# Batch 0's Z: filled by SBUF to SBUF transfers instead of through a DRAM scratch

## The chip, the cores and the metric

The kernel runs on one core of a Trainium2 chip. The metric is the device time of one execution in microseconds, as the median of several runs. Times inside the kernel come from one profiled execution and count from its first instruction. PE is TensorE, DVE is VectorE, ACT is ScalarE, POOL is GpSimd, SP is the queue that issues most transfers.

## The reference

`x` has 8 batches of 3008 rows and 256 columns. A frequency mixing is followed by an expert layer with ELU:

```python
X = np.fft.rfft(x, axis=1)
Yr = Xr @ w_r - Xi @ w_i + b_r
Yi = Xr @ w_i + Xi @ w_r + b_i
Y  = soft_threshold(Yr, 0.01) + 1j * soft_threshold(Yi, 0.01)
y  = np.fft.irfft(Y, n=3008, axis=1)
h  = y.reshape(8 * 3008, 256) @ w_in          # 256 x 2048
g  = np.where(h > 0, h, np.exp(np.minimum(h, 0)) - 1)
out = g @ w_out                               # 2048 x 256
```

## The kernel before

The sequence length is 3008 = 47 x 64. The forward transform of a batch has two steps. In step A, 64 rows of `x` (n2) for each of 47 column indices n1 are multiplied by the matrix `M1`; n1 is taken in 24 pairs (j and j + 23), one on each half of the 128 partitions, so that one product with `M1` gives 128 rows: a pair, two parts (32 cosine-like and 32 sine-like slots each). Six units A of four pairs each load their pairs from one of three tiles `xts` (two units a tile), write a PSUM tile and are copied to an SBUF tile `A` in bf16. In step X, a slot k of `Z` has the rows of all n1 on the partitions: `Z[p, k, :]`, and its product with `M2[:, k]` gives the frequencies in `XT`. Between the two, the axis n1 has to move from the free dimension to the partitions. That is done through a scratch in DRAM: unit A stores its tile to `DA` (L184 for batch 0, one store for each unit; L186 for the others), and `load_Z` (L192) reads `DA` back with 32 partitions a transfer, `Z[a:P:4]` for a = 0 to 2 (partitions with a = 3 are cleared once, by ACT, in `clear_Z`). For batch 0 the reads are cut at slots 8 and 16, so that the first units X (unit g, dt: 8 slots, one half of D) can start on the first slots.

Then come the units M (L254: four matmuls of `XT` with `wcat_r` and `wcat_s`, 128 rows of `Y` each; the bias comes through `bias_bc` or through a matmul with `bias_p` that starts the sum), the soft threshold (ACT Relu and DVE, or POOL), the inverse transform (B: L446, `DB` in DRAM, `Bs`, Y: L531), and the expert layer in blocks of 512 rows: front (L1032, L1044), ELU (L1083, L1073) and back (L1104).

All instructions of an engine run in the order in which the program writes them (a manual schedule). Batch 0's transform stands alone at the start; the transforms of the later batches are spread between the steps of the expert layer by `plan(b)`. The lines of the start, in program order:

- `idle_pe(n)` (L573) issues n matmuls on a constant that keep PE busy and whose result is not used.
- POOL issues the six loads of `x` for batch 0 (L118), SP those of `w_r`, `w_i` and the biases. Constants follow from iotas: `M1` (L689, L690 on DVE, of the Sin at L684), then `M2` in two halves g = 0, 1: `points`, `wraps`, `sizes`, `signs` on DVE (L731 to L761) and `sines` on ACT (L764); `slot0` (L776) scales M2's slot 0. `M3` follows from `v3`, `w3` and `a3` (L841 to L849 on DVE) by Sin on ACT (L917); POOL makes M4's inputs, `idm` and two casts of `wcat` (L780 to L801).
- `fA(u)` for u = 0 to 5: unit A of batch 0, then three idle matmuls. The PSUM tile of unit 5 is two banks (`apart`), copied by ACT and DVE.
- the seven `load_Z`, with the bias (through `bpd` in DRAM) between them; `idle_pe(26)`; the product that gives `bias_bc` (L854, L855).
- `load_w_in(0)` on SP; on POOL a `gate` that waits for a slot of Z, then the three loads of batch 1's `x` and half of `w_out` (L879).
- eight units X, evacuated by ACT (even) and DVE (odd, the last by both).
- `begin_M`, `first_M` and `fB` in a written order; `load_w_in(1)` is issued by SP after the store of `fB(3)`, and the scalings of `w_in` (L884) stand between the other steps of DVE.

Of the kernel before, what the change touches and what calls it, by code (L numbers as in the profile page):

```python
# [19 lines left out]
N1 = 47  # L20
# [9 lines left out]
def kernel(  # L30
# [112 lines left out]
    def evac(dst, src, on_dve):  # L143
        if on_dve:
            nc.vector.tensor_copy(dst, src)
        else:
            nc.scalar.copy(dst, src)  # L147

    def unit_A(b, u, alone=False, on_dve=False, apart=False):
# [12 lines left out]
        xt, A = xts[ci], A_of[b, ci]  # L162
        dav = DA_of[b].rearrange("j p d -> p j d")
# [6 lines left out]
        for j in range(2):  # L170
            nc.tensor.matmul(  # L171
                banks[j], lhsT=M1[:],
                rhs=xt[:, 4 * uu + 2 * j : 4 * uu + 2 * j + 2, :], start=True, stop=True,
            )
        Af = A[:, 4 * uu : 4 * uu + 4, :].rearrange("p n d -> p (n d)")
        if apart:
            for j in range(2):
                evac(Af[:, 512 * j : 512 * j + 512], banks[j], on_dve and bool(j))
        else:
            evac(Af, ps[:].rearrange("p a b -> p (a b)"), on_dve)  # L180
        j0 = 8 * ci
        if alone:
            j0 += 4 * uu
            nc.sync.dma_start(dav[:, j0 : j0 + 4, :], A[:, 4 * uu : 4 * uu + 4, :])  # L184
        elif uu == 1:
            nc.sync.dma_start(dav[:, j0 : j0 + 8, :], A[:])  # L186
# [7 lines left out]
    def unit_X(b, u, alone=False, on_dve=False, apart=False):  # L194
# [10 lines left out]
        for kk in range(8):  # L205
            k = 8 * g + kk
            nc.tensor.matmul(  # L207
                psv[kk // nk][:, kk % nk, 0 : 4 * K1], lhsT=Z[:, k, dt * P : dt * P + P],
                rhs=M2[:, k].rearrange("p c m -> p (c m)"), start=True, stop=True,
            )  # L210
# [365 lines left out]
    nc.vector.memset(bias_p[:], 0.0)  # L576
    bpd = dram.tile([3, 2 * D], BF16, name="bpd", tag="bpd")
# [5 lines left out]
    with tc.tile_pool(name="stagep", bufs=1) as stagep:  # L583
        def first_x(u):
            load_x(0, u // 2, 4 * (u % 2), 4 * (u % 2) + 4)
# [17 lines left out]
        w_r_f, w_i_f = (wk3.tile([P, 2, D], F32, name="yb", tag="yb") for _ in range(2))  # L603
        nc.sync.dma_start(w_r_f[:], w_r.rearrange("(c p) e -> p c e", p=P))
        nc.sync.dma_start(w_i_f[:], w_i.rearrange("(c p) e -> p c e", p=P))
        bsm = stagep.tile([8, D // 4], F32, name="bsm")
# [16 lines left out]
        def row(name, shape):  # L623
            return stagep.tile(shape, F32, name=name)
# [62 lines left out]
        c0 = col(dve, c1, -1.0, ALU.mult, 1.0, ALU.add)  # L687
        M1v = M1[:].rearrange("p (h k) -> p h k", h=2)
        dve.tensor_scalar(M1v[:, 0], r1[:], c0[:], None, ALU.mult)  # L689
        dve.tensor_scalar(M1v[:, 1], r1[:], c1[:], None, ALU.mult)  # L690

# [35 lines left out]

        def points(g):

            for t in range(2):  # L730
                dve.tensor_tensor(  # L731
                    v2[g][:, :, :, t], band(uw, t, 16 * g, 16),
                    kt[:, :, t].unsqueeze(1).to_broadcast([P, 16, K1]), ALU.add,
                )
# [43 lines left out]

        for k in range(3):
            pool.tensor_copy(bps[:, k], bsm[:])  # L780
            if k < 2:
                pool.tensor_tensor(bsm[:], bsm[:], bps[:, k], ALU.subtract)
        k4h = col(pool, qcol, 0.5, ALU.mult, -0.25, ALU.add)
# [3 lines left out]
        pool.tensor_tensor(c4[:], qcol[:], k42[:], ALU.subtract)  # L787
        nc.gpsimd.memset(lam_n[:], -LAM)
        nc.gpsimd.memset(hpi[:], 0.25 * TURN)
        ph4 = col(pool, c4, 0.25, ALU.mult, 0.25, ALU.add)  # L790
# [10 lines left out]
        pool.tensor_copy(wcat_s[:, :, D : 2 * D], w_r_f[:])  # L801

        def fA(u):
            unit_A(0, u, alone=True, on_dve=u == 5, apart=u == 5)
            if u < 5:
                idle_pe(3)

        points(0)
        wraps(0)
        sizes(0)  # L810
        signs(0)
        points(1)
        dve.tensor_scalar(m3i[:], m3i[:], 63, None, ALU.bitwise_and)
        k3 = row("k3", [P, NV])
        dve.scalar_tensor_tensor(k3[:], m3i[:], float(N1), k1t[:], ALU.mult, ALU.add)
        dve.tensor_scalar(sg3[:], k3[:], S // 2 + 0.5, -0.5, ALU.is_gt, ALU.add)
        full = [P, NV, N2]
        k3b = k3[:].unsqueeze(2).to_broadcast(full)
        for u in range(4):
            fA(u)  # L820
        nc.sync.dma_start(bpd[:].rearrange("k (q e) -> q k e", q=8), bps[:])
        fA(4)
        fA(5)
        ips.append(pre1.tile([P, 512], F32, name="ips", tag="mps1"))
        load_Z(0, 0, 0, 16)
        for k in range(3):
            nc.sync.dma_start(bias_p[32 * k : 32 * k + 1, :], bpd[k : k + 1, :])
        load_Z(0, 1, 0, 16)
        load_Z(0, 2, 0, 8)
        load_Z(0, 2, 8, 16)  # L830
        for a in range(3):
            load_Z(0, a, 16, NS)
        sines(0, 0)
        sines(0, 1)
        wraps(1)
        slot0()
        sines(1, 0)
        nc.scalar.activation(a2[1][:], v2[1][:], AF.Abs)
        nc.scalar.copy(wcat_r[:, :, D : 2 * D], w_i_f[:])
        nc.scalar.activation(wcat_s[:, :, 0:D], w_i_f[:], AF.Copy, scale=-1.0)  # L840
        dve.scalar_tensor_tensor(  # L841
            v3[:], n2row.unsqueeze(1).to_broadcast(full), 1.0 / S, k3b, ALU.mult, ALU.mult
        )
        signs(1)
        sines(1, 1)
        nc.scalar.activation(r4[:], v4[:], AF.Sin, bias=0.0, scale=TURN)
        dve.tensor_scalar(w3[:], v3[:], CMAGIC, -CMAGIC, ALU.add, ALU.add)
        dve.tensor_tensor(w3[:], v3[:], w3[:], ALU.subtract)
        dve.tensor_scalar(  # L849
            a3[:].bitcast(I32), w3[:].bitcast(I32), 0x7FFFFFFF, None, ALU.bitwise_and  # L850
        )
        nb = pre1.tile([P, 512], F32, name="ips", tag="mps1")
        idle_pe(26)
        nc.tensor.matmul(nb[:], lhsT=busy[:, 0:P], rhs=bias_p[:], start=True, stop=True)  # L854
        nc.scalar.copy(bias_bc[:], nb[:])  # L855

# [57 lines left out]
    for q, i in ((3, 0), (3, 1), (4, 1), (5, 1)):  # L914
        begin_M(q, i, pre2, "pre2")
    for o, src, sc, bi in ((1, w3, TURN, 0.0), (0, a3, -TURN, hpi[:])):
# [395 lines left out]
```

## Time and profile before

| | us |
|---|---|
| median of 3 runs (lowest, highest) | 879.21 (878.71, 880.23) |
| the profiled execution | 879.04 |
| its span, first to last instruction | 877.2 |
| PE busy | 862.8 (98%) |
| ACT busy | 713.9 (81%) |
| DVE busy | 664.2 (76%) |
| POOL busy | 583.4 (67%) |

A row of the timeline has the start, the length, the engine, the line, the operation, the tiles out and in, the shape and the count; in brackets stands the idle time of the engine before it and what ended it. Rows of the chain that ended last have start, length, engine, tile and line. Rows of groups have busy time and mean nanoseconds of one, then idle time before. Rows of stretches have from and to, the length, then busy time (and instructions) of PE, weight loads, DVE, ACT and POOL, the granted clock, the DMA share and GB/s.

### The profile page before, as it was taken

How to read it: one execution, taken by the hardware profiler on the slowest of the kernel's cores; microseconds unless marked ns; L12 is line 12 of the kernel's file. 1: busy time of each engine (PE TensorE's matmuls, PEld its weight loads, DVE VectorE, ACT ScalarE, POOL GpSimd, SP SyncE). 2: the span in 40 equal slices, each digit the busy share in tenths (PEclk: the TensorE clock that was granted, in tenths of full speed). 3: DMA queues.
4: the chain of work that ended last, by engine and by line, in shares of the span. 5: the costliest groups of instructions: out<-in, count | busy, mean ns of one | idle time of the engine just before them, and what ended most of it. 6: DMA issues, size and time to landing. Idle time of an engine off the chain costs nothing.

```text
span 877.2 us, 18462 instructions
## 1 busy us (share of the span) xinstructions
PE 862.8 (98%) x6731; PEld 670.2 (76%) x6731; DVE 664.2 (76%) x1106; ACT 713.9 (81%) x1248; POOL 583.4 (67%) x856
## 2 busy tenths in 40 slices
PE   7899999999999999999999999999999999999997
PEld 3467767877778877887778877787877878787776
DVE  7698778787776877768867788677777677788775
ACT  6777888888978889798887988879888798876664
POOL 7462550798757887578756888469874697734664
PEclk9999999999999999999999999999999999999999
DMA  8998337643383324733365532653337313250111
GB/s 255 330 260 239 98 96 200 186 133 85 97 264 122 97 73 122 240 121 108 89 179 162 162 104 79 176 175 128 101 82 229 87 33 91 73 145 25 38 37 49
DMA packets 118098, 117.69 MB, mean 134 GB/s; under 512 B 11651, under 2 KB 108934, under 8 KB 114486
## 3 DMA queue, kind: packets, MB, share of 16 engines
q1 hardware_dynamic: 111750, 88.97, 35.6%
q0 software_dynamic: 5968, 27.26, 9.8%
q8 instruction: 53, 0.87, 0.4%
q14 instruction: 39, 0.32, 0.1%
q10 hardware_dynamic: 288, 0.26, 0.1%
HBM read 54.86 MB, written 49.81 MB: 119 GB/s over the span
## 4 chain that ended last, share of the span: by engine, by line
PE 93%; POOL 2%; DVE 2%; ACT 1%; DMA 1%; SPq 1%; issue 0%; DVEq 0%; POOLq 0%
PE ps_o L1104 39%; PE hps L1032 33%; PE mps L296 5%; PE aps L171 2%; PE xps L207 2%; PE mps L1032 2%; PE yps L558 2%; PE bps L397 2%; PE mps L254 2%; PE sps L1032 1%; POOL Y L312 1%; DMA Z<-DA 1%; POOL yb L308 0%; PE ips L573 0%; POOL clip L311 0%; PE pre L254 0%
## 5 line engine op out<-in xcount | busy, mean ns | idle before, releaser
L1073 DVE SCALAR_TENSOR_TENSOR gT<-Et,hps 128x512 fp32r<-128x512 f32 x610 | 390.2, 683 | 135.7 <-POOL Et L1083 125.8
L1104 PE MATMUL ps_o<-w_out_r,gT 128*128 128x256 f32 x3008 | 477.3, 301 | 0.0
L1104 PEld LDWEIGHTS ps_o<-w_out_r,gT 128*128 128x128 f32 x3008 | 404.4, 189 | 48.2 <-DVE osb L1116 0.2
L1083 POOL TENSOR_SCALAR Et<-Et 128x512 f32<-128x512 f32 x482 | 288.0, 617 | 208.0 <-ACT Et L1044 206.3
L1032 PE MATMUL hps<-yT,w_in_s 128*128 128x512 bf16 (+7 forms) x1580 | 355.8, 352 | 0.9 <-DVE gT L1073 0.8
L1044 ACT ACTIVATE Et<-hps 128x512 f32<-128x512 f32 x494 | 271.5, 609 | 38.6 <-PE hps L1032 35.5
L1032 PEld LDWEIGHTS <-w_in_s 128*128 128x128 bf16 x1728 | 144.1, 98 | 104.9 <-issue 13.1
L1042 ACT ACTIVATE Et<-hps 128x512 f32<-128x512 f32 x192 | 104.5, 597 | 42.0 <-PE hps L1032 41.5
L1047 ACT ACTIVATE Et<-Et 128x512 f32<-128x512 f32 x192 | 110.5, 632 | 0.0
L312 POOL TENSOR_TENSOR Y<-yb,clip 128x512 bf16<-128x512 f32 x72 | 92.8, 1288 | 6.0
L308 POOL TENSOR_TENSOR yb<-yb,bias_bc 128x256 f32<-128x256 f32 x72 | 53.3, 740 | 11.2 <-DVE yb L303 11.2
L147 ACT CAST XT<-xps 128x768 bf16<-128x768 f32 x58 | 46.6, 805 | 15.9 <-PE xps L207 15.8
L303 DVE TENSOR_TENSOR yb<-mps,yb 128x512 f32<-128x512 f32 x72 | 49.8, 692 | 7.2
L147 ACT CAST yT<-yps 128x752 bf16<-128x752 f32 x56 | 44.1, 788 | 13.7 <-PE yps L558 13.5
L1075 DVE SCALAR_TENSOR_TENSOR gT<-hps,Et 128x512 fp32r<-128x512 f32 x78 | 50.2, 686 | 3.3
L147 ACT CAST A<-aps 128x1024 bf16<-128x1024 f32 x41 | 41.8, 1020 | 12.9 <-PE aps L171 11.0
L311 POOL TENSOR_SCALAR clip<-yb 128x512 f32<-128x512 f32 x72 | 44.3, 615 | 6.3
L147 ACT CAST Bz<-bps 128x1024 bf16<-128x1024 f32 x41 | 41.5, 1013 | 5.4 <-PE bps L397 5.1
L302 DVE TENSOR_TENSOR yb<-mps,bias_bc 128x256 f32<-128x256 f32 x72 | 30.5, 424 | 17.5 <-PE mps L296 15.7
L296 PE MATMUL mps<-wcat_s,XT 128*128 128x256 bf16 x288 | 43.2, 273 | 0.0
L1116 DVE COPY osb<-ps_o 128x512 f32<-128x512 f32 x46 | 31.7, 690 | 5.3 <-PE ps_o L1104 3.4
L224 POOL TENSOR_TENSOR XS<-XT 128x512 bf16<-128x512 bf16 x30 | 34.1, 1162 | 2.4 <-ACT XT L147 1.4
(201 smaller groups left out, 691.6 us busy)
## 6 DMA issues: line engine op xcount, KB each, us to landing
xt<-in_x_dram POOLq DMA_DIRECT2D x21, 1024.0 KB, 5.4
out_dram<-osb SPq DMA_DIRECT2D x158, 128.0 KB
Bs<-DB SPq DMA_DIRECT2D x30, 384.0 KB
Yx<-Y SPq DMA_DIRECT2D x168, 64.0 KB
DA<-A SPq DMA_DIRECT2D x19, 512.0 KB
DB<-Bz SPq DMA_DIRECT2D x19, 512.0 KB
Z<-DA SPq DMA_DIRECT2D x21, 384.0 KB
xt<-in_x_dram POOLq DMA_DIRECT2D x6, 512.0 KB, 8.2
```

Of the source, the lines that this page charges most:

```text
L147: nc.scalar.copy(dst, src)
L296: nc.tensor.matmul(out_, lhsT=lhs[:, dt] if lhs is not None else sum_of(dt, ch)[:, oc : oc + P], rhs=w[:, dt, :], start=(dt == 0), stop=(d ...
L308: nc.gpsimd.tensor_tensor(yb[:, D : 2 * D], yb[:, D : 2 * D], bias_bc[:, D : 2 * D], ALU.add)
L312: nc.gpsimd.tensor_tensor(Y_of[b, q][:, i, :], yb[:], clip[:], ALU.subtract)
L1032: nc.tensor.matmul(hps[s][:, c0:c1], lhsT=w_in_s[:, dt, ft * P : ft * P + P], rhs=yT_of[b][:, dt, t0 : t0 + c1 - c0], start=(dt == 0), sto ...
L1042: nc.scalar.activation(Et[:, s], hps[s], AF.Relu, scale=-1.0)
L1044: nc.scalar.activation(Et[:, s], hps[s], AF.Exp)
L1047: nc.scalar.activation(Et[:, s], Et[:, s], AF.Exp, scale=-1.0)
L1073: nc.vector.scalar_tensor_tensor(o, e, -1.0, h, ALU.add, ALU.max)
L1075: nc.vector.scalar_tensor_tensor(o, h, 0.0, e, ALU.max, ALU.add)
L1083: nc.gpsimd.tensor_scalar(e, e, 1.0, 0.0, ALU.min, ALU.max)
L1104: nc.tensor.matmul(po[q][:, i_ % 2, :], lhsT=gT[:, s, i_ * P : i_ * P + P], rhs=w_out_r[:, ft, :], start=(ft == 0 and i_ % 2 == 0), stop=( ...
```

## The change

- For batch 0, each unit A now multiplies by `M1c` instead of `M1`: a column pair's product is made by two accumulating matmuls of 256 columns, each with weights that are zero except on 64 of the 128 rows of the result, so that the two n1 pairs of a "t" share a PSUM bank by slots. A unit is eight matmuls of 256 columns instead of two of 512.
- The result of each half unit (t = 0, 1) goes from `A` straight into Z: `place(t)` writes 8 partitions (r0, r0 + 4, ... r0 + 28), 32 slots of 256 each, from 128 partitions of 512 elements. SP issues one of the two, POOL the other. `DA`, its stores and the seven `load_Z` are gone for batch 0; the slots of Z are interleaved for it, which `unit_X` undoes by its index.
- Every slot of Z now needs all twelve transfers; the `gate` before batch 1's loads is gone. `M1`, for the later batches, is made by two ACT instructions.
- Around it the start is rewritten: idle matmuls 1 (3 after unit 1) between the units and 16 after them; `w_r` and `w_i` are loaded after the placements; the bias goes from SBUF to `bias_p` without `bpd`; `w3` moves from DVE to POOL, in front of batch 1's loads; `sines(1, 1)` moves behind the first unit X; the `w_i` parts of `wcat` and `bias_bc` move behind the units X; the Sin of `r4` moves behind the first units M; the last unit X uses one tile.

The diff, cut to what matters:

```diff
-            if ci == 0:
+            if ci == 0 and not alone:
                 DA_of[b] = dram.tile([NJ, P, D], BF16, name="DA", tag="DA")
...
+        if alone:
+            for t in range(2):
+                for q in range(2):
+                    for j in range(2):
+                        nc.tensor.matmul(
+                            banks[t][:, D * q : D * q + D],
+                            lhsT=M1c_of[0][:, q, N2 - N2 * j : N2 - N2 * j + P],
+                            rhs=xt[:, 4 * uu + 2 * t + j, :], start=(j == 0), stop=(j == 1),
+                        )
...
+        def place(t):
+            r0 = 16 * (4 * uu + 2 * t) + ci
+            eng = nc.gpsimd if t == by_pool else nc.sync
+            eng.dma_start(Z[r0 : r0 + 29 : 4], Af[:, 512 * t : 512 * t + 512])
+
+        by_pool = 0 if apart else 1
...
-        if alone:
-            j0 += 4 * uu
-            nc.sync.dma_start(dav[:, j0 : j0 + 4, :], A[:, 4 * uu : 4 * uu + 4, :])
...
-                lhsT=Z[:, k, dt * P : dt * P + P],
+                lhsT=Z[:, k if b else 2 * (k % 16) + k // 16, dt * P : dt * P + P],
...
-        if b == 0:
+        if b == 0 and (q, i) != (3, 0):
             todo.sort(key=lambda z: z[1])
...
+        M1c = stagep.tile([P, 2, 3 * N2], F32R, name="M1c")
+        nc.vector.memset(M1c[:].bitcast(F32), 0.0)
...
+        r1v = r1[:].rearrange("p (q a b) -> p q a b", q=2, a=2)
+        for h, c in enumerate((c0, c1)):
+            dve.tensor_scalar(
+                M1c[:, :, N2 + NS * h : N2 + NS * h + NS].rearrange("p a (q b) -> p a q b", q=2),
+                r1v, c[:], None, ALU.mult,
+            )
...
+        def fA(u):
+            unit_A(0, u, alone=True, on_dve=u == 5, apart=u == 5)
+            if u < 5:
+                idle_pe(3 if u == 1 else 1)
...
+        points(1, (0,))
+        for u in range(3):
+            fA(u)
+            split_bias(u)
+            if u == 1:
+                for h, c in enumerate((c0, c1)):
+                    nc.scalar.activation(M1[:, N2 * h : N2 * h + N2], r1[:], AF.Copy, scale=c[:])
+        fA(3)
         k4h = col(pool, qcol, 0.5, ALU.mult, -0.25, ALU.add)
         k4 = col(pool, k4h, CMAGIC, ALU.add, -CMAGIC, ALU.add)
         k42 = col(pool, k4, 2.0, ALU.mult)
+        fA(4)
+        fA(5)
         c4 = stagep.tile([P, 1], F32, name="c4z")
         pool.tensor_tensor(c4[:], qcol[:], k42[:], ALU.subtract)
...
         pool.tensor_scalar(idm[:], prow, pcol[:], None, ALU.is_equal)
+        ips.append(pre1.tile([P, 512], F32, name="ips", tag="mps1"))
+        nc.sync.dma_start(w_r_f[:], w_r.rearrange("(c p) e -> p c e", p=P))
+        nc.sync.dma_start(w_i_f[:], w_i.rearrange("(c p) e -> p c e", p=P))
         pool.tensor_copy(wcat_r[:, :, 0:D], w_r_f[:])
         pool.tensor_copy(wcat_s[:, :, D : 2 * D], w_r_f[:])
...
         for k in range(3):
-            nc.sync.dma_start(bias_p[32 * k : 32 * k + 1, :], bpd[k : k + 1, :])
...
+            nc.sync.dma_start(bias_p[32 * k : 32 * k + 1, :], bps[:, k])
+        points(1, (1,))
         sines(0, 0)
         sines(0, 1)
         wraps(1)
+        sizes(1)
         slot0()
         sines(1, 0)
...
         signs(1)
...
-        idle_pe(26)
...
+        idle_pe(16)
...
     load_w_in(0)
-    gate(Z[:, 8, 0:1])
+    nc.gpsimd.tensor_scalar(w3[:], v3[:], CMAGIC, -CMAGIC, ALU.add, ALU.add)
+    nc.gpsimd.tensor_tensor(w3[:], v3[:], w3[:], ALU.subtract)
     for ci in range(3):
         load_x(1, ci)
     load_w_out(0)
     for u in range(8):
-        unit_X(0, u, alone=True, on_dve=u % 2, apart=u == 7)
+        unit_X(0, u, alone=True, on_dve=u % 2)
         if u < 3:
             idle_pe(1)
+        if u == 0:
+            sines(1, 1)
+    nc.scalar.copy(wcat_r[:, :, D : 2 * D], w_i_f[:])
+    nc.vector.tensor_scalar(wcat_s[:, :, 0:D], w_i_f[:], -1.0, None, ALU.mult)
...
     for q, i in ((3, 0), (3, 1), (4, 1), (5, 1)):
         begin_M(q, i, pre2, "pre2")
+    nb = pre1.tile([P, 512], F32, name="mps1", tag="mps1")
+    nc.tensor.matmul(nb[:], lhsT=busy[:, 0:P], rhs=bias_p[:], start=True, stop=True)
+    nc.scalar.copy(bias_bc[:], nb[:])
+    nc.vector.tensor_scalar(
+        a3[:].bitcast(I32), w3[:].bitcast(I32), 0x7FFFFFFF, None, ALU.bitwise_and
+    )
...
     first_M(4, 0, False)
+    nc.scalar.activation(r4[:], v4[:], AF.Sin, bias=0.0, scale=TURN)
```

More of the change, by code (lines that the diff above doesn't have):

```diff
@@ L147, in evac @@
             nc.scalar.copy(dst, src)
+    M1c_of = []
     def unit_A(b, u, alone=False, on_dve=False, apart=False):
@@ L169, in unit_A @@
             banks = [ps[:, j, :] for j in range(2)]
[L170 to L175, printed above, removed]
+        if alone:
[7 more added lines that the diff above has]
+                        )
+        else:
+            for j in range(2):
+                nc.tensor.matmul(
+                    banks[j], lhsT=M1[:],
+                    rhs=xt[:, 4 * uu + 2 * j : 4 * uu + 2 * j + 2, :], start=True, stop=True,
+                )
[4 more added lines that the diff above has]
+        by_pool = 0 if apart else 1
         if apart:
@@ L726, in band, with points @@
             )
-        def points(g):
-            for t in range(2):
+        def points(g, ts=(0, 1)):
+            for t in ts:
                 dve.tensor_tensor(
@@ L776, in slot0, with split_bias @@
                     dve.tensor_scalar(w, w, cc[:], None, ALU.mult)
-        for k in range(3):
+        nc.gpsimd.memset(lam_n[:], -LAM)
+        nc.gpsimd.memset(hpi[:], 0.25 * TURN)
+        def split_bias(k):
             pool.tensor_copy(bps[:, k], bsm[:])
@@ L782 @@
                 pool.tensor_tensor(bsm[:], bsm[:], bps[:, k], ALU.subtract)
+        def fA(u):
+            unit_A(0, u, alone=True, on_dve=u == 5, apart=u == 5)
+            if u < 5:
+                idle_pe(3 if u == 1 else 1)
+        points(0)
+        wraps(0)
+        sizes(0)
+        signs(0)
+        dve.tensor_scalar(m3i[:], m3i[:], 63, None, ALU.bitwise_and)
+        k3 = row("k3", [P, NV])
+        dve.scalar_tensor_tensor(k3[:], m3i[:], float(N1), k1t[:], ALU.mult, ALU.add)
+        dve.tensor_scalar(sg3[:], k3[:], S // 2 + 0.5, -0.5, ALU.is_gt, ALU.add)
+        full = [P, NV, N2]
+        k3b = k3[:].unsqueeze(2).to_broadcast(full)
+        dve.scalar_tensor_tensor(
+            v3[:], n2row.unsqueeze(1).to_broadcast(full), 1.0 / S, k3b, ALU.mult, ALU.mult
+        )
+        points(1, (0,))
[6 more added lines that the diff above has]
+        fA(3)
         k4h = col(pool, qcol, 0.5, ALU.mult, -0.25, ALU.add)
```

68 lines of the change are left out of this document (14 added, 54 removed).

## The prediction

> **What bounds the kernel now.** I read the page first (the chain by engine), then the busy time by stretches, then the chain of the first 60 us, and last the timeline of the stages that the diff touches.
>
> ```profile
> span 877.2 us, 18462 instructions
> ...
> PE 93%; POOL 2%; DVE 2%; ACT 1%; DMA 1%; SPq 1%; issue 0%; DVEq 0%; POOLq 0%
> 24.00:31.00 7.00, 4.51 (x71) 3.30 (x69) 3.96 (x6) 4.20 (x7) 2.94 (x5) 1.00 0.83 265
> ...
> 31.00:44.00 13.00, 13.00 (x93) 5.84 (x91) 8.57 (x14) 10.36 (x18) 7.50 (x8) 1.00 1.19 380
> ...
> 100.00:800.00 700.00, 699.82 (x5558) 557.69 (x5556) 531.25 (x859) 594.00 (x1038) 485.62 (x675) 1.00 0.44 127
> ```
>
> The first numbers of each stretch are its length and the busy time of PE. From 100 to 800 us PE is full; the diff changes nothing there, so whatever the start wins or loses arrives at the end. The start has one hole: 2.5 us of PE between 24 and 31. From 31 to 44 PE is full and the DMA engines are too (share 1.19, 380 GB/s). The profiled execution took 879.04 us, of which 877.2 are the span; the median of the three runs is 879.21. I sum against 879.04. A measurement of this kernel can tell about 0.2% (1.76 us) from no change.
>
> ```profile
> 10.99 0.85 PE aps L171 x2
> ...
> 11.84 1.31 PE ips L573 x3
> ...
> 14.80 0.47 PE aps L171 x2
> ...
> 23.65 4.56 DMA Z<-DA
> ...
> 53.51 0.94 PE ps_o L1104 x8
> ```
>
> These are rows of the chain: start, length, what. Batch 0's Z is the hole: the last read back from DRAM ends at 28.2.
>
> **The A products.** A unit was two fp32 matmuls of 512 columns, 0.85 us at half clock and 0.47 at full; it becomes eight of 256, twice the columns. At full clock eight such matmuls with eight weight loads take 0.94 (last row), so 0.47 more; at half clock 1.7 by the same doubling. Idle matmuls fall from three to one (three after the second unit), 0.44 each at half clock and 0.22 at full.
>
> ```profile
> 8.49 1.19 PE L171 MATMUL aps<-xt,M 128*128 128x512 f32 x2 [3.02 <-DVE v L731]
> ...
> 13.80 1.00 PE L573 MATMUL ips<-busy 128*128 128x512 bf16 x3
> ...
> 17.34 0.59 ACT L147 CAST A<-mps 128x512 bf16<-128x512 f32 x1
> ...
> 17.65 0.69 DVE L145 CAST A<-mps 128x512 bf16<-128x512 f32 x1 [3.80 <-PE mps L171]
> 2.98 0.75 POOL L118 DMA_DIRECT2D xt<-in_x_dram  x1
> ```
>
> Start 8.49; w_r and w_i (0.5 MB) no longer travel ahead of x, which I count as 0.3 us (between 0 and 0.5). So 8.2; unit 0 to 9.9, idle to 10.3, unit 1 to 12.0, three idles to 13.3; the clock rises near 14 (three idles in 1.00 instead of 1.31); unit 2 to 14.4, then 0.94 + 0.22 each: the sixth ends at 17.9. Its halves leave PSUM by ACT at 18.4 and by DVE at 18.65, against 17.93 and 18.34 now. If half-clock weight loads do not hide, this is up to 0.9 later; PE could also be 0.3 earlier. The zeroing of M1c (about 0.4) hides on DVE before the Sin at 3.93, which ACT's clearing of Z holds back anyway; the two scalings that now make M1 are small and fall in idle time of ACT.
>
> **Z.** Gone: six stores to DRAM, seven reads back. New: twelve transfers of 128 KB, six issued by SP, six by POOL (0.75 us each, as the x loads). POOL's last waits for ACT at 18.4 and ends at 19.2.
>
> ```profile
> q1 hardware_dynamic: 576, 0.26, 18.1%
> q1 hardware_dynamic: 317, 0.29, 27.6%
> DMA to landing us min/median/max: 5.1/6.2/11.8
> DMA to landing us min/median/max: 7.6/7.6/7.6
> ```
>
> The queue rows give packets, MB and share of 16 engines. The first is 107 to 113 us, Yx alone, SBUF to SBUF in 512 B: 0.181 x 6 x 16 / 512 = 34 ns a packet (the other 64 carry semaphores). The second, 92 to 96 us, is stores of 1 KB, 62 ns. A placement is 128 packets of 1 KB, 34 to 62 ns each; I take 55. Nothing in the trace shows one that writes eight partitions. The third row is all 27 loads of x: 5.1 us at best for 1 MB, of which 2.6 are bytes at about 400 GB/s, so 2.5 fixed. Over eight engines a placement moves in 16 x 55 ns = 0.9, so the last lands 18.5 + 2.5 + 0.9 = 21.9; over sixteen 21.5; if it waits as the last Z read does now (4.56), 23.2.
>
> The Trainium skill, "DMA: Bandwidth & Descriptors", section "Why a DMA increments its semaphore by 16 and not by 1", says that a transfer is spread over the largest number of engines, up to 16, that divides the slowest dimension of both sides. For eight partitions that is eight engines, and on SP's queue always the lowest eight; the sum by it is the 21.9 just given, and no printed row here shows the engines one by one.
>
> **M2 and X.** X now needs all of Z at once, and M2's zero slot.
>
> ```profile
> 12.23 1.02 DVE L731 TENSOR_TENSOR v<-uw,kt 128x384 f32<-128x384 f32 x2
> ...
> 18.26 0.55 DVE L741 TENSOR_SCALAR r<-v 128x768 f32<-128x768 f32 x1
> ...
> 18.84 0.96 DVE L742 TENSOR_TENSOR v<-v,r 128x768 f32<-128x768 f32 x1
> ...
> 19.78 0.66 DVE L776 TENSOR_SCALAR M<-M,c 128x24 bf16<-128x24 bf16 x4
> ...
> 21.45 1.15 DVE L761 SCALAR_TENSOR_TENSOR a<-a,c,sw 128x384 f32<-128x384 f32 x2
> ...
> 24.09 0.56 DVE L849 TENSOR_SCALAR A<-A 128x768 int32<-128x768 int32 x1
> ...
> 24.49 0.80 ACT L147 CAST XT<-xps 128x768 bf16<-128x768 f32 x1
> ...
> 24.96 0.96 DVE L145 CAST XT<-xps 128x768 bf16<-128x768 f32 x1 [0.30 <-PE xps L207]
> ...
> 30.27 0.50 ACT L147 CAST XT<-mps 128x384 bf16<-128x384 f32 x1
> ...
> 31.08 0.38 PE L254 MATMUL pre<-wcat_r,XT 128*128 128x512 bf16 x1
> ```
>
> DVE after 18.65: half of the points (0.5), wraps (0.55 + 0.96), sizes (0.56), slot0 (0.8 with its column): 22.0. The sixteen idles (3.5 us from 18.4) end then too, and Z lands at 21.9, so X starts at 22.1. DVE does the signs (1.15) until 23.2 and then four copies of 0.96; ACT four of 0.80 and a sine between. Both end near 27.3, limited by three PSUM buffers and these copies. M starts at 27.6 after wcat_r, against 31.08: **3.4 us** on PE.
>
> **What is late next.** On ACT, the w_i copy, bias_bc and r4's sine now stand between X and the later work: its clip of (4,1), at 35.11 now, moves to about 33.0, 2.1 earlier. PE then waits some 0.3 us at each B step (the first is at 35.49) for Y of the units before, so about **2.3** of the 3.4 is left at 38.
>
> Then comes a transfer. `w_in_f(1)` is issued right behind the first DB store, and the DVE scaling of it ends a wait:
>
> ```profile
> 25.90 0.66 POOL L118 DMA_DIRECT2D xt<-in_x_dram  x1 [0.35 <-PE xps L207]
> ...
> 35.11 0.67 ACT L337 ACTIVATE clip<-pre,lam_n 128x512 f32<-128x512 f32 x1
> ...
> 35.49 0.61 PE L446 MATMUL pre<-Y,M 64*128 64x256 bf16 x8
> ...
> 37.23 0.39 SPq L462 DMA_DIRECT2D DB<-Bz  x1
> ...
> 43.82 0.60 DVE L884 TENSOR_SCALAR w_in_s<-w_in_f 128x512 bf16<-128x512 f32 x1 [0.80 <-DMA w_in_f<-in_moe_w_in_dram]
> ```
>
> Ahead of it in the saturated engines are batch 1's x (3.1 MB) and half of w_out (1.0), so it lands when their bytes are through, however early it is issued. Behind it on DVE stand the Y steps of the last units, which PE's last B products and first_Y wait for. Hence the date of POOL's x loads decides. Now the first is issued at 25.90 and lands 7.6 later (the last of the four rows above, that load alone), at 33.5.
>
> ```profile
> 12.49 0.34 POOL L787 TENSOR_TENSOR c4z<-c,c 128x1 f32<-128x1 f32 x1
> ...
> 17.01 0.60 POOL L801 CAST wcat_s<-yb 128x512 bf16<-128x512 f32 x1
> L1083 POOL TENSOR_SCALAR Et<-Et 128x512 f32<-128x512 f32 x482 | 288.0, 617 | 208.0 <-ACT Et L1044 206.3
> L312 POOL TENSOR_TENSOR Y<-yb,clip 128x512 bf16<-128x512 f32 x72 | 92.8, 1288 | 6.0
> 9.30 0.96 DVE L742 TENSOR_TENSOR v<-v,r 128x768 f32<-128x768 f32 x1
> 9.43 0.98 POOL L782 TENSOR_TENSOR bsm<-bsm,bps 8x64 f32<-8x64 f32 x1
> ```
>
> After: POOL is free of placements at 19.2; the string from c4z to the wcat casts takes 5.1 now (12.49 to 17.61), 4.8 without what has moved ahead; w3 is new there: 617 and 1288 ns per 512 columns make 0.93 + 1.93 for 768. So x is issued at 26.9. Z and w_in_f(0) are through by then, so it lands after 5.1, the row's best: 32.0, **1.5 us** earlier. That, not the 2.3, is what arrives behind 43.82, since what follows in the queue is the same bytes. With x issued between 26.1 and 28.1 it is 2.3 (then compute decides) to 0.3.
>
> One rule weighs on this. POOL's subtract of 8x64 took 0.98 us and ended at 10.41, just after DVE's two-input subtract of 9.30 to 10.26. The Trainium skill, "SBUF — State Buffer", section "SBUF: two separate sides", says that a DVE operation with two SBUF inputs locks out a GpSimd one that reads SBUF for its whole length. That row agrees, and it is the third rival's ground.
>
> **The sum.** 879.04 - 1.5 = 877.5. From 50 us on I count nothing: the later loads of w_in and w_out(1) are issued relative to the same work, and PE is full.
>
> **The rivals.** *Nothing binds at 43.82* (DMA through sooner because x loads start on idle engines, the A phase quicker): then PE's gain arrives almost whole, 2.5 to 3.2, at 876.2. For it: DVE's wait at 43.82 is only 0.8. *POOL is held up*: its subtract for w3 and its short string run beside DVE's wraps and signs (0.96 + 1.15); 2 us of lock puts x at 28.9, landing 34.0, and the gain is gone: 879.3 with what DVE then waits more. *Z lands late*, slower: if all twelve placements run on the same eight engines at 62 ns, they need 12 x 16 x 62 ns = 11.9 us of them, behind the x loads that hold these engines until about 14.5. Z is then there at 26.4 with the landing, X 4.3 later than 22.1, which eats the 2.1 that ACT has at 35 and 2.2 more: 881.2. It decides from about 24.2 on. Against it: six of them can move before 15 us, in share with x, and POOL's may use other engines.
>
> **How the numbers follow.** Forecast 0.55, its own range 876.7 to 878.7 (gains of 2.3 to 0.3), of which 0.31 lie below 877.45, the bound for faster. Nothing binds 0.15, faster. POOL held up 0.12, within. Z late 0.18, slower. So faster 0.46, same 0.36, slower 0.18. For 8 in 10 the range runs from 876.0 to 880.2: it leaves out the end of the first rival and the larger half of the last.
>
> **What the profile after would show.** A units of eight matmuls in 0.94 us at full clock; the last evacuation near 18.5; first X matmul near 22.1 with DVE slot0 or Z as releaser; XT complete near 27.3; first M matmul near 27.6; x of batch 1 issued near 26.9 and landed near 32.0; w_in_f(1) still waited for by DVE, near 42.3. I am wrong in the sign if X starts after 24.2, and in the size if DVE does not wait for w_in_f(1) or POOL issues x after 28.

## The result, and the profile after

The changed kernel is slower: 881.92 us in the median of 7 runs (879.59 to 882.75), against 878.40 for the kernel before (7 runs, 876.07 to 880.23). The ratio is 1.0033, with a 95% interval of 1.0016 to 1.0049, so the change costs about 3 us where I had forecast a gain of 1.5. The profiled execution has a span of 880.1 us, against 877.2.

The chain of waits of the changed kernel, from the last A product to the end of the start (start, length, what):

```profile
15.61 0.69 DVE A L145
...
16.32 6.86 DMA Z<-A
...
23.42 0.50 PE xps L229 x8
...
29.93 1.02 PE pre L349 x4
...
42.14 5.54 DMA DB<-Bz
...
47.87 3.31 DMA Bs<-DB
...
51.27 0.83 PE one L554 x16
```

The last half of A leaves PSUM at 15.61 instead of 17.65, 2 us sooner than before. Then the chain is on transfers for 7 us until X starts at 23.42. The second stretch on transfers (the DB store and the Bs read back, 42.14 to 51.18) is new: before, no transfer stood in the chain between 28 and 53 us.

The busy time by stretches says where TensorE lost it (length, busy time of PE, PEld, DVE, ACT, POOL, then granted clock, DMA share, GB/s):

```profile
24.00:31.00 7.00, 5.94 (x64) 4.50 (x63) 4.64 (x6) 4.41 (x6) 6.92 (x7) 0.76 0.05 15
31.00:44.00 13.00, 12.47 (x72) 5.45 (x70) 9.16 (x13) 10.41 (x18) 8.13 (x10) 1.00 1.14 372
44.00:50.00 6.00, 4.84 (x91) 3.43 (x90) 4.61 (x11) 4.35 (x12) 2.97 (x5) 1.00 0.55 150
50.00:60.00 10.00, 8.67 (x58) 5.13 (x59) 7.97 (x15) 7.51 (x16) 4.42 (x7) 1.00 1.11 317
```

and the last of these stretches in the kernel before:

```profile
50.00:60.00 10.00, 9.96 (x54) 5.88 (x51) 8.99 (x16) 8.75 (x18) 6.58 (x10) 1.00 1.11 296
```

The first row points to the cause. Between 24 and 31 us the DMA engines are almost idle (share 0.05, before 0.83), while GpSimd is busy for 6.92 of 7.00 us. TensorE's 5.94 there look better than the 4.51 of before, but they were run at a granted clock of 0.76. What was not transferred then is transferred later: 0.53 us of PE are lost between 31 and 44, and the 1.33 us idle between 50 and 60 stand where there were 0.04. GpSimd's timeline in that stretch:

```profile
23.84 0.61 POOL L860 CAST wcat_r<-yb 128x512 bf16<-128x512 f32 x1 [1.15 <-DMA yb<-in_w_r_dram]
24.40 0.61 POOL L861 CAST wcat_s<-yb 128x512 bf16<-128x512 f32 x1
24.97 2.80 POOL L916 TENSOR_SCALAR A<-Bz 128x768 f32<-128x768 f32 x1
27.86 1.81 POOL L917 TENSOR_TENSOR A<-Bz,A 128x768 f32<-128x768 f32 x1
29.60 1.97 POOL L118 DMA_DIRECT2D xt<-in_x_dram  x3
```

GpSimd first waits 1.15 us for w_r, which now goes out on SyncE behind the placements, and then spends 4.6 us on w3. Batch 1's x loads go out at 29.60, 3.7 us later than the 25.90 of before, and the first of them lands at 35.03, 1.5 us later than the 33.53 of before.

### The profile page after: what moved, and what is told of

Read it like the earlier page. It is cut to its first block, busy times and chain, and to the rows that moved or that the text cites. A ratio compares the mean times of both kernels' runs of the same rounds, so it can differ in the third digit from the quotient of the medians.

```text
span 880.1 us, 18508 instructions
## 1 busy us (share of the span) xinstructions
PE 862.9 (98%) x6749; PEld 675.5 (77%) x6749; DVE 665.2 (76%) x1107; ACT 712.3 (81%) x1247; POOL 590.3 (67%) x863
## 4 chain that ended last, share of the span: by engine, by line
PE 91%; POOL 3%; DMA 2%; DVE 2%; ACT 1%; issue 0%; DVEq 0%; POOLq 0%; SPq 0%
PE ps_o L1133 38%; PE hps L1061 33%; PE mps L319 5%; PE xps L229 3%; PE mps L1061 2%; PE yps L581 2%; PE bps L420 2%; PE aps L183 2%; PE mps L277 1%; DMA DB<-Bz 1%; POOL Y L335 1%; DMA Z<-A 1%; DMA Bs<-DB 1%; PE aps L176 1%; PE sps L1061 1%; DVE gT L1102 1%
## 5 line engine op out<-in xcount | busy, mean ns | idle before, releaser
L147 ACT CAST XT<-xps 128x768 bf16<-128x768 f32 x58 | 46.6, 804 | 19.2 <-PE xps L229 18.9
L229 PE MATMUL xps<-M,Z 128*128 128x96 bf16 x512 | 33.7, 212 | 4.0 <-DMA Z<-A 3.8
```

The source lines that it names most:

```text
L229: nc.tensor.matmul(psv[kk // nk][:, kk % nk, 0 : 4 * K1], lhsT=Z[:, k if b else 2 * (k % 16) + k // 16, dt * P : dt * P + P], rhs=M2[:, k] ...
```

## The experiments

I held two theories. *Late loads*: the 3 us are the lateness of batch 1's x and w_out, which move the whole saturated DMA stretch. *Slow X*: Z lands late (eight engines), TensorE idles, and X runs at a lowered clock.

One table carries most of the reading. Its dates are those of single profiled executions: the first M product on PE, the first x load of batch 1 on GpSimd, and ACT's first Et step, the landmark by which the start is over (from it to the 51st Et step all runs go in step to 0.05 us). "Bs gap" is the time from ACT's 51st Et step to the first yps product of batch 1. The last column has the median and, estimated from all timed runs and not from the medians, the ratio to the kernel before with its interval. In the experiments the kernel before was timed beside each run; its medians are 877.93 to 878.36.

| run | M starts | x issued | first Et step | Bs gap | median us, ratio (95%) |
|---|---|---|---|---|---|
| before, the profile predicted from | 31.08 | 25.90 | 74.19 | 7.50 | |
| before, again (b2) | 29.56 | 24.02 | 72.67 | 7.55 | |
| after | 31.00 | 29.60 | 76.57 | 8.33 | 881.92, 1.0033 (1.0016 to 1.0049) |
| e1 w3 on VectorE | 29.40 | 23.59 | 73.43 | 8.26 | 879.84, 1.0013 (1.0001 to 1.0025) |
| e2 33 idle matmuls | 28.89 | 28.02 | 76.26 | 8.91 | 882.29, 1.0048 (1.0031 to 1.0066) |
| e3 all on GpSimd | 33.45 | 31.19 | 78.07 | 8.94 | 883.10, 1.0048 (1.0031 to 1.0066) |
| e4 all on SyncE | 30.86 | 29.29 | 75.55 | 8.28 | 880.60, 1.0025 (1.0010 to 1.0039) |
| e5 before, w_r later | 29.32 | 24.35 | 73.13 | 7.62 | 878.09, 1.0000 (0.9987 to 1.0012) |
| e7 three repairs | 29.14 | 24.67 | 73.05 | 8.61 | 879.06, 1.0009 (0.9998 to 1.0019) |
| e8 before, w3 on GpSimd | 29.23 | 28.09 | 75.04 | 7.54 | 879.72, 1.0017 (1.0003 to 1.0030) |
| e9 e7 + DRAM slots | 28.72 | 23.85 | 72.62 | 8.71 | 878.46, 1.0002 (0.9993 to 1.0012) |
| e10 e9, all on SyncE | 31.61 | 20.90 | 75.51 | 9.00 | 881.52, 1.0037 (1.0022 to 1.0052) |
| e11 before, 20 matmuls more | 30.34 | 24.10 | 73.40 | 8.14 | 878.82, 1.0006 (0.9995 to 1.0016) |
| e12 e7, 24 matmuls more | 28.89 | 24.29 | 72.87 | 8.05 | 878.57, 1.0002 (0.9991 to 1.0013) |

**e1: w3 back on VectorE.**

```diff
+        dve.tensor_scalar(w3[:], v3[:], CMAGIC, -CMAGIC, ALU.add, ALU.add)
+        dve.tensor_tensor(w3[:], v3[:], w3[:], ALU.subtract)
         idle_pe(16)
...
-    nc.gpsimd.tensor_scalar(w3[:], v3[:], CMAGIC, -CMAGIC, ALU.add, ALU.add)
-    nc.gpsimd.tensor_tensor(w3[:], v3[:], w3[:], ALU.subtract)
```

> The changed kernel with one thing undone: the two steps of w3 are back on VectorE, behind the signs, so GpSimd issues batch 1's x right behind its two wcat casts, near 25.0 us instead of 29.6. Theory 'late loads' (the loss of 3 us is the 3.7 us by which batch 1's x and w_out are issued later than before): first x load of batch 1 issued near 25.0 and landed near 30.5, the Bs load landed near 48.3 instead of 51.2, time 879.0 or less, that is 2.5 to 3 us under the changed kernel. Theory 'slow X' (X starts late and runs at a clock of 0.76): X is as late as in the changed kernel, so the time stays at 881 to 882. If only half of the 3 us comes back, both hold a part.

x goes out at 23.59, the Bs read is issued at 43.73 instead of 47.87 and is not waited for, and the first Et step comes 3.1 us sooner. In the times 0.13% over the kernel before are left of 0.33%: 1.8 of the 2.9 us come back, so two lines of the change made more than half of its loss. GpSimd's casts began 1.4 us earlier too (22.48, without the wait for w_r), and X at 21.74 instead of 23.42, so e1 alone does not clear *slow X*; e2 and e8 have to.

**e2: 33 idle matmuls.**

```diff
-        idle_pe(16)
+        idle_pe(33)
```

> The changed kernel with 33 idle matmuls ahead of X instead of 16, which should keep TensorE busy until 23.3 us, when Z has landed. Theory 'slow X': the granted clock between 24 and 31 us is near 1.00 instead of 0.76, the last XT copy ends 0.5 to 1.5 us earlier, and the time falls by as much, to 880.5 to 881.5. Theory 'late loads': the clock and XT change as said, but x of batch 1 is issued at 29.6 as before and the time stays within 0.4 us of the changed kernel.

By stretches, and the waits of 40 to 53 us (what waited for what: total, times, longest):

```profile
24.00:31.00 7.00, 5.63 (x61) 3.49 (x59) 5.03 (x7) 5.28 (x8) 6.92 (x6) 1.00 0.19 40
...
44.00:50.00 6.00, 3.23 (x44) 2.43 (x45) 3.70 (x10) 1.45 (x6) 1.16 (x2) 0.73 0.47 130
```

```profile
DVE w_in_s L901 <- DMA w_in_f<-in_moe_w_in_dram: 3.5, 1, 3.5
```

The clock of X is 1.00 and M starts 2.1 us earlier than in the changed kernel, yet the time is no better. The 2.1 us turn into a longer wait of VectorE for w_in_f(1), 3.5 us where the changed kernel has 1.2, and behind it TensorE is busy for only 3.23 of 6 us, at a granted clock of 0.73. X's date and clock alone bring nothing back here, so *slow X* falls as the cause of the 3 us. The test is not clean on the other side: x went out at 28.02 in this execution, 1.6 us earlier than in the changed kernel and not at 29.6 as I expected, and that too brought only 0.3 us at the first Et step.

**e8: w3 on GpSimd in the kernel before.** The counter-test: no placement, only the late loads.

```diff
     gate(Z[:, 8, 0:1])
+    nc.gpsimd.tensor_scalar(w3[:], v3[:], CMAGIC, -CMAGIC, ALU.add, ALU.add)
+    nc.gpsimd.tensor_tensor(w3[:], v3[:], w3[:], ALU.subtract)
     for ci in range(3):
         load_x(1, ci)
```

(and the two VectorE steps taken out, a3 moved behind X as in the change.)

> The kernel before with one part of the change alone: w3's two steps go from VectorE to GpSimd, between its gate on Z and batch 1's x loads. No placement is in it, and Z is as before. Theory 'late loads': x of batch 1 is issued near 28.7 to 29.7 us instead of 25.9, the first w_in_f wait and the Bs load move by nearly as much, TensorE waits for Bs near 50, and the time is 2 to 3 us over the kernel before, 880.2 to 881.2. Rival (the placements themselves cost the 3 us): the time stays within 0.5 us of 878.2.

```profile
23.30 0.19 POOL L887 CAST gate<-Z 128x1 f32<-128x1 bf16 x1 [4.30 <-DMA Z<-DA]
23.44 2.81 POOL L895 TENSOR_SCALAR A<-Bz 128x768 f32<-128x768 f32 x1
...
28.09 1.90 POOL L118 DMA_DIRECT2D xt<-in_x_dram  x3
```

```profile
DVE w_in_s L879 <- DMA w_in_f<-in_moe_w_in_dram: 2.3, 1, 2.3
```

The wait grows to 2.3 us without any placement (0.8 and 0.5 in the two profiles of the kernel before), and the time rises by 0.17% (1.5 us, interval 0.03% to 0.30%). That is less than the 2 to 3 I expected, TensorE does not wait for Bs as I had expected, and the lower end of the interval does not exclude the rival's 0.5 us; the first Et step, 2.4 us later than in b2, speaks for the theory.

The row also settles a dispute of the prediction. w3's first step took 2.79 to 2.82 us in every run that had it on GpSimd, here with nothing on VectorE beside it but copies out of PSUM. So it was not held up by VectorE; that is its own length, 3.6 ns a column. On VectorE the same step takes 0.55 us (L847 of before). The kernel before has another GpSimd row at that rate, the scaling of w_in, one multiplication of 256 columns (least, median and most ns, then first and last start):

```profile
L884 POOL TENSOR_SCALAR w_in_s<-w_in_f x2: 852/858/865, 55.7 to 58.0; 128x256 bf16<-128x256 f32 x2
```

That is 3.3 ns a column, where the row that I had scaled (L1083, a min and a max by constants) takes 1.2.

**e5: the kernel before with w_r and w_i behind x.** The two loads (0.5 MB) are issued by GpSimd behind batch 0's x.

```diff
-        nc.sync.dma_start(w_r_f[:], w_r.rearrange("(c p) e -> p c e", p=P))
-        nc.sync.dma_start(w_i_f[:], w_i.rearrange("(c p) e -> p c e", p=P))
...
+        nc.gpsimd.dma_start(w_r_f[:], w_r.rearrange("(c p) e -> p c e", p=P))
+        nc.gpsimd.dma_start(w_i_f[:], w_i.rearrange("(c p) e -> p c e", p=P))
         for k in range(3):
             pool.tensor_copy(bps[:, k], bsm[:])
```

> The kernel before with one part of the change alone: the loads of w_r and w_i (0.5 MB) leave SyncE's queue ahead of x and are issued by GpSimd behind batch 0's x loads. In the changed kernel the first x load lands 2.4 us earlier than before, and I lay that to this move. By that the first A product starts near 6.1 us instead of 8.5, the last A copy ends near 16, Z is read back 1.5 to 2.4 us earlier, the hole ahead of X shrinks, and the time is 877 or less (1 to 2 us faster than before). Rival: the early start comes from something else in the change (the zeroing order, GpSimd's shorter list), then the first A product stays at 8.5 and the time at 878.4 to 879. Second rival: the A phase is earlier but the date of batch 1's x loads decides; they wait for Z here, so part of the gain arrives, 0.5 to 1.5.

The first A products, e5 above and the kernel before (b2) below:

```profile
5.90 0.70 PE L171 MATMUL aps<-xt,M 128*128 128x512 f32 x2 [0.75 <-DVE c L593]
```

```profile
7.83 0.71 PE L171 MATMUL aps<-xt,M 128*128 128x512 f32 x2 [2.36 <-DMA xt<-in_x_dram]
```

The early start does come from this move: 1.9 us between these two. Over all profiles the first A product starts at 7.34 to 8.49 in the four with w_r and w_i ahead of x, and at 5.71 to 6.12 in the ten without. Nothing of it arrives in the time, because the DA stores and Z reads that follow take it back: the last Z read is issued at 21.85, against 21.91 in b2.

**e3 and e4: who issues the placements.** In e3 GpSimd all twelve, in e4 SyncE (`eng = nc.sync`).

```diff
-            eng = nc.gpsimd if t == by_pool else nc.sync
+            eng = nc.gpsimd
```

> The changed kernel with all twelve placements of Z issued by GpSimd. Theory 'eight engines' (a transfer that writes eight partitions uses eight engines, SyncE's always the same eight): GpSimd's transfers take turns over all sixteen, so the bytes of Z are through sooner, Z complete near 21 instead of 23.2, and X starts near 21.5. Rival: the placements are slow per packet wherever they run, and GpSimd issues six more at some 0.7 us each, 4 us more, so Z is complete no earlier than 23 and x of batch 1 is issued later than 29.6. As x of batch 1 waits for w_r and w3 on GpSimd in either case, the time stays at 881 to 882.5 by the theory 'late loads', and falls by 1 to 2 us by 'slow X' if Z is earlier.

> The changed kernel with all twelve placements of Z issued by SyncE. Theory 'eight engines': they all run on the same eight engines, so the hardware queue's share of the sixteen engines between 18 and 22 us stays near one half (0.40 to 0.50) while placements alone are left, 12 x 16 x 60 ns = 11.5 us of each of the eight, Z is complete near 25 to 26 instead of 23.2. Rival: the placements spread over all sixteen; then the share goes to 0.7 or more and Z is complete by 22. The time: GpSimd loses six issues, but its wcat casts wait for w_r, which lies behind the placements on SyncE, so x of batch 1 is issued no earlier than 29 and the time is 881 to 884 by the theory, 880.5 to 882 by the rival.

e4, 14 to 17 us, where placements are all that moves (packets, MB, share of sixteen engines):

```profile
q1 hardware_dynamic: 579, 0.56, 54.1%
```

0.541 x 16 = 8.7 engines are busy; the packets of the placements take 47 ns. The trace also has eight landings for each of SyncE's placements. So these do run on eight engines. The Trainium skill, "DMA: Bandwidth & Descriptors", section "Why a DMA increments its semaphore by 16 and not by 1", spreads a transfer over the largest number of engines that divides both slowest dimensions; this row agrees for eight partitions. My expected 25 to 26 us for Z in e4 was still wrong, since it took 60 ns a packet: the last placement lands at 22.75 and X starts at 23.21, no later than in the changed kernel. In e3 the rival was right, not the theory of an earlier Z: GpSimd issues its last placement at 21.2, and Z lands 3.9 us later:

```profile
21.21 3.93 DMA Z<-A
25.23 0.80 PE xps L229 x8
```

So GpSimd alone is later still: its last issue comes 5.2 us after the last copy of A (16.03), because steps of its own (17.26 to 19.11) stand in front of the last four issues.

**e7: three repairs together.** e1, with w_r and w_i on GpSimd as in e5, and idle_pe(33).

> Three repairs of the changed kernel together: w3's two steps on VectorE, w_r and w_i issued by GpSimd behind batch 0's x loads, 33 idle matmuls ahead of X. Theory 'late loads': the wcat casts no longer wait for w_r, x of batch 1 is issued near 22 to 23.5 us, Z is complete near 21.5 to 23, and no Bs load is waited for ahead of 50 us; time 878.5 to 879.5, since the first repair alone gave 879.8 and the other two remove only a wait of 1.2 us and a clock of 0.84 to 0.94 around 24. Rival: the earlier x loads meet the last placements on the DMA engines and delay Z by 1 us or more; then 880 or more. The placements are worth having only if this beats the kernel before with w_r moved alone (878.1).

M starts at 29.14 and x at 24.67 (later than the 22 to 23.5 expected), both as in e5, and the first Et step is as in e5 (73.05 against 73.13). With everything around them mended, the placements bring M no sooner than the DRAM scratch does, and the time is 0.09% over the kernel before (-0.02% to 0.19%).

**e9, e10: DRAM slots, and x as early as it can be.** All kernels of the change lose a second piece at 143 us, where TensorE waits for batch 1's Bs. e9 sets the two dropped DRAM buffers aside again:

```diff
-            if ci == 0 and not alone:
+            if ci == 0:
                 DA_of[b] = dram.tile([NJ, P, D], BF16, name="DA", tag="DA")
...
+    bpd = dram.tile([3, 2 * D], BF16, name="bpd", tag="bpd")
```

> The three repairs, with the two DRAM scratch buffers that the change drops (batch 0's DA, the bias buffer) set aside again but not used, so that batch 1's DA and DB lie where they lie in the kernel before. All runs with the change so far lose 0.75 us more at 143 us, where TensorE waits for batch 1's Bs load (the first yps product comes 8.3 us after ACT's 51st Et step instead of 7.55), and none without it does, whatever their dates. Theory 'place in DRAM': the distance is 7.5 to 7.6 again and the time falls by 0.75 to about 878.3. Rival (something else in the order of batch 1): the distance stays at 8.3 to 8.6 and the time at 879.1.

The gap stays (8.71): the place in DRAM is not the cause. The time, 878.46, comes close to the theory's 878.3 all the same, with the gap still there. e10 is e9 with all placements on SyncE and idle_pe(24):

> The repairs and the DRAM slots as in e9, with all twelve placements on SyncE and 24 idle matmuls. GpSimd then has no placements to issue and its casts no wait, so x of batch 1 is issued near 20 us. Theory 'late loads' at its limit: Z is complete near 21.5, M starts near 28, w_in_f(1) and Bs are not waited for, and the time is 877.5 to 878.3, level with the kernel before or 0.5 under it. Rival: the early x loads share the engines with the last placements, Z comes at 23 or later and the time is 878.5 to 880.

x goes out at 20.90, but Z, over SyncE's eight engines alone, comes later (the last placement lands at 23.61, in e7 at 22.31), X starts at 24.07, runs at a granted clock of 0.76, and M starts at 31.61. The time is 881.5. So a late M costs about as much as a late x: the first Et step goes roughly with whichever of the two is later (table: x at 24 and M at 29 give 72.6 to 73.4; x at 28 with M at 29 gives 75.0 to 76.3; x at 21 with M at 31.6 gives 75.5).

**b2: the kernel before, profiled again.**

> The kernel before, profiled again. The profiled execution that I predicted from took 879.04, 1 us over the median of the runs since (878.0). If its start was slower than usual (first A product at 8.49, where a later run with the same front began at 7.3), this one begins near 7.3 and M near 30 instead of 31.08. If not, it begins at 8.4 to 8.5 again and the difference lies later.

```profile
24.02 0.66 POOL L118 DMA_DIRECT2D xt<-in_x_dram  x1 [0.35 <-PE xps L207]
```

```profile
29.56 0.38 PE L254 MATMUL pre<-wcat_r,XT 128*128 128x512 bf16 x1
```

A begins 0.66 us earlier than in the profile that I predicted from, x is issued 1.9 and M starts 1.5 us earlier. One execution's dates in the start vary that much.

**e11, e12: the second piece.** The trace has 16 KB packets of queue q8, instructions, one at a time. In the runs of the kernel before with its own program for TensorE one falls 10 us behind ACT's 51st Et step, clear of the DB-to-Bs round trip (1 to 8 us behind that step); in all runs of the change but e12 it falls inside, at 6 or at 2 us. TensorE's program is longer there: eight matmuls for two in each A unit. e11 lengthens it in the kernel before; e12 does the same on e7, with 28 idle matmuls for 33 and 29 short ones.

```diff
-        idle_pe(26)
+        idle_pe(21)
+        for _ in range(25):
+            nc.tensor.matmul(ips[-1][:, 0:16], lhsT=busy[:, 0:P], rhs=busy[:, 0:16], start=True, stop=True)
```

> The kernel before, with 25 matmuls of 16 columns in the place of 5 of the 26 idle matmuls ahead of X: the same idle time, 20 matmuls more in TensorE's program. In the traces so far one 16 KB packet of queue q8 (instructions) falls near 10 us after ACT's 51st Et step in the runs that keep the early part of the kernel before (954 weight loads by then), near 6 us in those with 972 to 975, near 2 us in those with 980 to 992; and those of the last two kinds wait at 143 us for batch 1's Bs load, by 0.75 and 1.1 to 1.4 us. Theory 'instruction packet': with 974 weight loads the packet falls near 6 us here too, the first yps product comes 8.3 us after that step instead of 7.55, and the time is 0.7 us over the kernel before. Rival (the wait comes from something else that the change does to batch 1): the distance stays at 7.5 to 7.6.

> The three repairs, with 28 idle matmuls and 29 of 16 columns ahead of X instead of 33 idle ones: the same idle time, 24 matmuls more. Theory 'instruction packet': with some 1015 weight loads it falls before the DB stores of that round trip begin (1 us after the 51st Et step or sooner), the first yps product is back at 7.5 to 7.6 us after it instead of 8.6, and the time falls by 1 us to 878.0 or a little less. Rival: the distance stays at 8.3 to 8.7 and the time at 879.0.

The packet in e11 (140 to 142 us: packets, MB, share), and its waits:

```profile
q8 instruction: 1, 0.02, 3.4%
```

```profile
PE yps L558 <- DMA Bs<-DB: 0.5, 1, 0.5
```

and 142 to 146 us in e7 and in e12:

```profile
142.00:146.00 4.00, 3.05 (x34) 2.47 (x33) 2.79 (x6) 2.54 (x5) 0.00 (x0) 1.00 1.00 270
```

```profile
142.00:146.00 4.00, 3.89 (x38) 2.99 (x39) 3.56 (x7) 3.29 (x6) 0.00 (x0) 1.00 0.98 262
```

e11 goes as the theory has it: twenty matmuls more bring the packet to 5.8 us and the wait into a kernel that never had it. In e12, 24 more than in e7 move the packet to 1.0 us ahead of the 51st Et step, the wait for Bs is gone and TensorE's loss in the window falls from 0.95 to 0.11 us. The packet occupies one DMA engine for about 1 us (0.034 x 2 us x 16). But e12's gap is 8.05, hardly less than the 8.14 of e11 and not the expected 7.55: 0.3 us of it are lost before the 53rd Et step (2.14 us behind the 51st, 1.82 in all other runs), and the rest I have not traced. In the times the two steps (+0.06%, -0.05 to 0.16; and 1.0009 to 1.0002) have the right sign and stay within the scatter. So that the packet's place brings the wait for Bs and takes it away is shown in the traces; what it costs in time is not.

None of these versions beats the kernel before.

## Why the prediction was wrong, point by point

- **What decides.** I wrote "the date of POOL's x loads decides", and for x this late that holds: e1 and e8 move the time by it in both kernels. The forecast fell with the date: 26.9 predicted, 29.60 measured, of which the step below made 1.9 us and the wait for w_r most of the rest. From issue to landing it was right (5.4 us, 5.1 predicted). My own condition ("in the size if ... POOL issues x after 28") named it; that it would carry the sign I had priced too low. My rule of one us in the time for each us at the landing, added to the median of the kernel before and counted from the landing in a usual execution (31.79 in b2), comes near in e8 (33.36: 879.5, measured 879.72), e4 (34.54: 880.7, 880.60), e3 (36.63: 883.0, 883.10) and the changed kernel (35.03: 881.6, 881.92), without the second piece, and fails in e2 (33.67: 880.1, 882.29).
- **w3 on GpSimd, the term that failed.** I took 0.93 + 1.93 us. The second step came as sized (1.81); the first took 2.80, three times its price. I scaled a TENSOR_SCALAR of the same engine (L1083, 617 ns for 512 columns) without asking what it computes: a min and a max, where w3's step makes two additions. The trace of before held nearer neighbours: the scaling of w_in (L884), 0.85 us for 256 columns, which makes 2.6 for 768, and the two additions of r4 (L797), 0.43 us for only 47 columns. The number of operations does not tell these rows apart (L1083 has two, L884 one); that their kind does is what the rows suggest, and no run isolates it.
- **GpSimd's string.** It ran from 17.58 to 25.0, not 19.2 to 24.0. It was ready at 22.7 and then waited 1.15 us for w_r, which I had let "no longer travel ahead of x" without asking when it would land behind the placements instead. That wait varies between executions: in e1 and e2, with the same order of loads, the casts began at 22.48 and 22.26 without it, in e4 it was 4.9 us.
- **The A phase.** 0.3 us (0 to 0.5) predicted for the w_r and w_i loads; e5 measures 1.9. The sixth unit ended near 15.6 instead of 17.9. This error was in my favour and was spent in waiting for Z.
- **Z.** Eight engines were right (e4). The landing was not: with the last SyncE placement issued by 16.9, Z was complete at 23.18, where my fixed time and eight engines behind GpSimd's last issue (17.6 + 2.5 + 0.9) give 21. GpSimd's and SyncE's placements together used 0.70 of the engines between 16 and 18 us (rows of 41.0% and 28.6%). I predicted 21.9 and gave 23.2 as the bound. GpSimd's placements moved in packets of 4 KB (215 ns each between 16 and 18 us), not in the 1 KB that I had assumed for all.
- **X and the clock.** Sixteen idle matmuls ended at 19.6, not with Z. After 3.83 us of idle TensorE X ran at 0.76 and XT ended near 29.9 instead of 27.3; of the 3.4 us on PE nothing was left at M (31.00 against 31.08). I had not costed the idle time at all. It did not matter here (e2); in e10, with x early, it came on top of a late Z: X again ran at 0.76 and took 6.4 us to its last copy, 5.2 in e7 at 1.00.
- **The base.** My sum measured gains against 31.08 and 25.90. In b2 these dates are 29.56 and 24.02; e5 and e8 agree in M (29.32 and 29.23), e11 lies between (30.34). The 3.4 us would have been 2.0 against a usual execution, before any other error.
- **The second piece.** "From 50 us on I count nothing" was wrong by 0.8 us at 143 us; e11 and e12 lay the wait there to TensorE's longer program.
- **The rivals.** *POOL is held up* came nearest: x at 28.9 by it, against 29.60. Its reason was wrong (the step was long by itself), and its 879.3 was 2.6 us too low: 0.8 of that is the second piece, and for the rest it counted the lateness of x as 0.5 us at the landing, where the first Et step shows that more than half of it arrives (e8: x 4.1 us later than in b2, the step 2.4; changed kernel: 5.6 and 3.9). The rule that I leaned on there, the Trainium skill's "SBUF — State Buffer", section "SBUF: two separate sides", did not come into play in this row: in all five runs VectorE had only copies out of PSUM beside it. A row of e3 agrees with the rule: GpSimd's cast of 8x64 took 0.87 us beside a two-input step of VectorE (12.76 to 13.71) and 0.23 elsewhere in that run. *Z lands late* was not the cause in the changed kernel, but e10 shows its price when x is early: X at 24.07 and 3.2 us over the kernel before.

The account: from b2 to the changed kernel the first Et step moves by 3.9 us. e1, which gives x its date, takes back 3.1; the three repairs and a usual execution take back the rest (72.6 to 73.1, against 72.67). The gap at 143 us adds 0.8. That makes 4.7, and the spans of the two profiles differ by only 3.8, because b2 loses 0.7 us of TensorE between 760 and 780 us, where it waits for a transfer of Yx and the changed kernel does not. What stays open: at M e9 is 0.8 us ahead of b2 and at the first Et step level with it. TensorE's busy time between 31 and 44 us (12.42 against 12.86) says that half of this is lost at once in waits, and the other half I have not traced.

## What to carry to other kernels

Follow an added step on a side engine to the transfers that this engine issues behind it: here 4.6 us of arithmetic in front of three DMA issues cost about 1.5 us (e8), and the removed DRAM round trip gained nothing even with that and the rest mended (e7, e9). Size a step by a row of the same engine that computes the same operations, not only by one of the same form, and ask of a load that is moved out of the way where it lands then. And profile the base a second time before measuring gains against its dates: in a stretch led by transfers they differed by 1.5 us between two executions of the same kernel.

## What the runs showed of the hardware

- On GpSimd a TENSOR_SCALAR of two additions took 2.79 to 2.82 us for 128x768 f32 in five profiles, 3.6 ns a column (0.55 us on VectorE); one multiplication took 0.85 for 128x256, f32 to bf16, 3.3 ns a column; a min and a max took 0.617 for 128x512, 1.2 ns a column.
- Transfers of 128 KB into eight partitions, issued by SyncE, kept 8.7 of sixteen DMA engines busy, at 47 ns for a packet of 1 KB, and had eight landings each (e4, e10).
- With two loads (0.5 MB together) issued first on SyncE's queue, the first A product, which needs GpSimd's first x load, started at 7.34 to 8.49; without them at 5.71 to 6.12.
- After 3.6 to 3.8 us of idle TensorE the granted clock was 0.76 between 24 and 31 us (the changed kernel and e10); with idle matmuls up to X it was 1.00 (e2, e7).
- A longer program of TensorE moved a 16 KB instruction packet in time (9.8 to 5.8 us behind the 51st Et step in e11). In the runs where it falls into the DRAM round trip, the gap is 0.6 to 1.5 us longer than the 7.55 of b2 (e11 8.14, e10 9.00).
